# A new order of all queues in the opening fifth of a fused kernel: gated linear attention, then a feed-forward with hardswish

## The chip, the core and the metric

The kernel runs on one core of one Trainium2 chip. The core has five engines that run side by side and meet through semaphores: PE (TensorE, matmuls, with its weight loads as PEld), DVE (VectorE), ACT (ScalarE), POOL (GpSimd) and SP (SyncE, which here issues every DMA). Each engine takes its instructions strictly in the order in which the program gives them. The metric is the device time of one execution in microseconds (us); lower is better.

## The reference

The first block is a linear recurrence with a gate, for 4 batches x 8 heads, 768 steps, head size 48. Its output, seen as 3072 tokens x 384, goes through two matrices with hardswish between them. All inputs are float64 or float32 as given; the result is float32.

```python
def _attn_ref(q, k, v, alpha) -> np.ndarray:
    ...
    for t in range(S):
        state = alpha[:, :, t, :, None] * state + np.einsum('bhd,bhe->bhde', k[:, :, t], v[:, :, t])
        y[:, :, t] = np.einsum('bhd,bhde->bhe', q[:, :, t], state)
...
def _moe_ref(x, w_in, w_out) -> np.ndarray:
    h = x @ w_in                      # 3072 x 384 by 384 x 2048
    relu6 = np.clip(h + 3.0, 0.0, 6.0)
    g = h * relu6 / 6.0
    return (g @ w_out).astype(np.float32)
```

## The kernel before

**Tiling.** The sequence is cut into 24 chunks j of 128 tokens, six to a batch. Two chunks make a group g of 256 tokens, the unit of the feed-forward; there are 12 groups. The decay within a chunk is turned into scans along time, after which a chunk needs masked scores, a product with v, and a state carried to the next chunk. Groups 0 and 1 use plain matmuls for the first matrix (steps f, fa, fb), group 0 for the second too (b); from group 1's second matrix (steps s, x, P, K, G) and group 2's first matrix (steps y, xc, M, n, o) on, products of sums of blocks take their place, with fewer matmuls and more additions on DVE. The sums of weight blocks (x for w2, y for w1) are made once, in place, near the end of the opening.

**Steps and order.** All work is written as small functions, each under a short name in the dictionary `steps` (line 729), and one long list of words, passed to `run` (line 745), calls them one after the other: `d3.6` is `high_bits(6)`. Under the manual schedule an engine's queue is the order of that list, restricted to the instructions for that engine. Dependencies (a tile read after it was written, a buffer written again after its last reader) become semaphore waits, at which the whole queue behind them stands.

**The steps that matter here**, with the engine and the line of their costly instruction in the kernel before:

- Loads on SP: la, lk, lq (alpha, k, q of a chunk; L251 for chunks 0 to 5, into three ring buffers each; L262, four DMAs a chunk, from chunk 6 on, into two buffers "quads" each), lv (v, two DMAs, L272), w (one of 16 slices of the two weight matrices, L162 or L166).
- Weights, slice i: d2 (ACT, L196), d1 (ACT, L186), dx (ACT, L191, slices 0, 1, 2, 4 alone), d3 (DVE, two or three instructions: L203 and L205, or L207, L208 and L210), d4 (POOL, L217, which reads what d3, d1 and dx wrote). A slice's raw buffer is loaded again for a later slice once its d4 has read it.
- Chunk j: ta, tk, tq are PE transposes (L282) for chunks 0 to 5; from chunk 6 on tk, tq and ca are 32x32 transposes on DVE (L286). ca places alpha (ACT, L300, chunks 0 to 5), r and p are the scans (DVE, L309 and L320), k and q multiply (DVE, L332; out of PSUM for chunks 0 to 5, out of SBUF from 6 on), kb and ck turn k on PE and copy it (L374, L378), sc and m are scores and mask (PE L346, DVE L356), u, sm, st, sv the state (PE L429, DVE L439, POOL L409, ACT L419), qa places q (ACT, L366), ya, yb, cy the output of attention (PE L455, ACT L464).
- Feed-forward: f, fa, fb (PE, L478 and L489), fr and fg the gate (ACT L494, DVE L498), b (PE, L516), bo and so copy and store it; s (DVE, L647 and L664) and x (DVE, L647) are sums, P (PE, L703) the products, K and G copies and sums of them (ACT L682, DVE L719 or ACT L716), O the stores (L724); y (DVE, L537 to L541), xc (same lines), M (PE, L600), n (ACT, L606), o (DVE).
- z issues matmuls of the identity whose result nobody reads (PE, L532).

**Buffers.** Eight PSUM banks: t0 to t3 for attention, m0 to m3 for the feed-forward; the last number of a PE step's word is its bank, and a bank is free once ACT or DVE has read it. Three raw buffers (and two borrowed ones for slices 3 and 4) hold weight slices; sums y overwrite them later.

**Padding.** From chunk 6 on, loads into a quads buffer leave a corner of 32 x 64 elements of two partition blocks unwritten. The first load of each of the six buffers (a, k, q, two each) sets it to 1.0 with two memsets on POOL (L257), just ahead of its DMAs.

Of the kernel before, what the change touches and what calls it, by code (L numbers as in the profile page):

```python
# [17 lines left out]
def kernel(  # L18
# [228 lines left out]

    def load_akq(name, j):
        src = rows({"a": alpha, "k": k, "q": q}[name], j)
        if j < FIRST:  # L250
# [4 lines left out]
        if j < FIRST + NQ:
            for o in (BLK, 3 * BLK):
                nc.gpsimd.memset(to[o : o + BLK, :, V - 1, D - BLK : BLK], 1.0)  # L257
# [463 lines left out]
    def store2(g, i):  # L721
# [8 lines left out]
        "lq": lambda j: load_akq("q", j), "lv": load_v, "w": load_weight,  # L730
# [19 lines left out]
    with tc.manual_schedule():  # L750
        run("""z.0.5 z.0.3 z.0.1 z.0.8 qa.0.0 w.0 d2.0 d3.0 la.0 ta.0.0 ca.0 r.0 lk.0 tk.0.1 k.0
               z.0.2 p.0 la.1 ta.1.2 lq.0 tq.0.3 ca.1 r.1 lk.1 lv.0.0 sv.0.0 d1.0 kb.0.0 ck.0 z.0.2
               u.0.2.1 sm.0.0 sv.0.1 q.0 qa.0.1 tk.1.0 k.1 p.1 z.0.2 sc.0.2.3 m.0 la.2 ta.2.0 ca.2
# [179 lines left out]
```

## Time and profile before

| | us |
|---|---|
| Median of 3 runs | 533.65 |
| Lowest and highest | 533.3 and 533.85 |
| The profiled execution's own time | 533.84 |
| Its span, first to last instruction | 531.8 |
| PE busy | 522.2 |
| DVE busy | 477.0 |
| ACT busy | 257.4 |
| POOL busy | 50.4 |

A row of the timeline gives the start in us from the span's start, the duration in us, engine, line, operation, tiles, shape and count; in square brackets stands how long the engine had been idle before it and what ended that. In the chain the columns are start, duration and what. "PE m_ps L600" is a matmul into a bank of the feed-forward, issued in line 600. A matmul's duration includes its way through the array, so rows overlap; the distance between starts is what PE needs for one.

The profile names lines, not steps. Since every engine keeps the order of the list, the n-th instruction of an engine in the trace belongs to the n-th in the program, and so each row can be given its step.

### The profile page before, as it was taken

The page shows a single profiled execution, that of the slowest core. Times are in us where ns is not written, and L with a number is a line of the kernel's source. Part 1 is how long each engine was busy: PE and PEld are TensorE (multiplying, and loading weights), DVE is VectorE, ACT ScalarE, POOL GpSimd, SP SyncE. Part 2 cuts the span into 40 slices and gives each one's busy share as a digit, 9 for nine tenths or more (in the row PEclk, how much of TensorE's full clock was granted, in tenths as well). Part 3 has the DMA queues.
Part 4 walks back from the last instruction along what each step waited for, and adds up shares of the span by engine and source line. Part 5 has one row for each costly group of instructions (what it writes and reads, how often), then busy time and mean ns, then how long its engine had stood idle before and what let it go on. Part 6 is the DMA issues. An engine that isn't in the chain of part 4 may idle for free.

```text
span 531.8 us, 15143 instructions
## 1 busy us (share of the span) xinstructions
PE 522.2 (98%) x6306; PEld 496.9 (93%) x6306; DVE 477.0 (90%) x849; ACT 257.4 (48%) x503; POOL 50.4 (9%) x71
## 2 busy tenths in 40 slices
PE   7799999999999999999999999999999999999997
PEld 7698886789999999999999999999999999999997
DVE  6999989999999999999999999999999899496382
ACT  3889865212653553553544444642634544553340
POOL 5333425100000000000000000000000000000000
PEclk9999999999999999999999999999999999999999
DMA  9998887006615156254345356055364052100001
GB/s 173 218 254 247 211 231 156 18 2 149 155 31 118 30 125 139 49 137 100 89 107 118 90 123 143 18 134 111 92 138 105 10 110 44 44 2 2 15 16 37
DMA packets 124100, 54.40 MB, mean 102 GB/s; under 512 B 83328, under 2 KB 116864, under 8 KB 124032
## 3 DMA queue, kind: packets, MB, share of 16 engines
q1 hardware_dynamic: 124032, 53.44, 44.0%
q8 instruction: 49, 0.80, 0.7%
q14 instruction: 19, 0.16, 0.1%
HBM read 44.50 MB, written 8.91 MB: 100 GB/s over the span
## 4 chain that ended last, share of the span: by engine, by line
PE 81%; DVE 9%; ACT 3%; DMA 3%; POOL 2%; issue 1%; SPq 0%; DVEq 0%; POOLq 0%; ACTq 0%
PE m_ps L703 34%; PE m_ps L600 34%; PE m_ps L478 4%; PE t_ps L455 3%; PE t_ps L346 2%; PE t_ps L429 2%; DMA v<-in_v_dram 1%; DMA raw<-in_moe_w_out_dram 1%; DVE rings L647 1%; DVE R L309 1%; DVE raw L537 1%; ACT raw L186 1%; DVE g_sb L647 1%; ACT raw L191 1%; DVE w L537 1%
## 5 line engine op out<-in xcount | busy, mean ns | idle before, releaser
L606 ACT COPY g_sb<-m_ps 128x512 f32<-128x512 f32 x110 | 63.6, 584 | 123.7 <-PE m_ps L600 104.3
L703 PE MATMUL m_ps<-w,g_sb 128*128 128x192 f32 x704 | 121.7, 327 | 0.0
L703 PEld LDWEIGHTS m_ps<-w,g_sb 128*128 128x128 f32 x704 | 113.7, 190 | 0.4
L703 PE MATMUL m_ps<-rings,g_sb 128*128 128x192 f32 x528 | 91.5, 326 | 0.0
L703 PEld LDWEIGHTS m_ps<-rings,g_sb 128*128 128x128 f32 x528 | 85.4, 190 | 0.1
L600 PE MATMUL m_ps<-xc,w 128*128 128x128 f32 x640 | 82.8, 277 | 0.4 <-DVE w L541 0.4
L600 PEld LDWEIGHTS m_ps<-xc,w 128*128 128x128 f32 x640 | 77.5, 192 | 1.7 <-issue 0.6
L494 ACT ACTIVATE r<-g_sb,half 128x512 f32<-128x512 f32 x80 | 56.8, 722 | 33.1 <-DVE g_sb L541 12.1
L498 DVE SCALAR_TENSOR_TENSOR g_sb<-r,g_sb 128x512 f32<-128x512 f32 x80 | 53.7, 683 | 4.3 <-ACT r L494 3.9
L600 PE MATMUL m_ps<-xT,raw 128*128 128x128 f32 x400 | 52.5, 277 | 0.0
L600 PEld LDWEIGHTS m_ps<-xT,raw 128*128 128x128 f32 x400 | 48.6, 192 | 0.6
L409 POOL TENSOR_TENSOR st<-sm,R 128x192 f32<-128x192 f32 x20 | 12.9, 643 | 352.2 <-DVE sm L439 305.5
L647 DVE TENSOR_TENSOR g_sb<-g_sb 128x512 f32<-128x512 f32 (+1 forms) x55 | 41.9, 792 | 0.2
L600 PE MATMUL m_ps<-xT,w 128*128 128x128 f32 x320 | 42.0, 276 | 0.0
L600 PEld LDWEIGHTS m_ps<-xT,w 128*128 128x128 f32 x320 | 39.3, 192 | 0.1
L366 ACT COPY A<-q 48x256 f32<-48x256 f32 x88 | 35.6, 404 | 5.0 <-DVE q L332 3.8
L356 DVE TENSOR_TENSOR A<-t_ps,mask 64x256 f32<-64x256 f32 x96 | 36.0, 413 | 0.4
L478 PE MATMUL m_ps<-xT,w 128*128 128x256 f32 x144 | 32.8, 382 | 0.1
L600 PE MATMUL m_ps<-xc,raw 128*128 128x128 f32 x240 | 31.8, 276 | 0.0
L309 DVE TENSOR_TENSOR_SCAN R<-t,ones 128x516 f32<-128x516 f32 x24 | 29.6, 1235 | 1.0 <-ACT t L300 0.9
L478 PEld LDWEIGHTS m_ps<-xT,w 128*128 128x128 f32 x144 | 26.7, 190 | 3.8 <-POOL w L217 0.2
L600 PEld LDWEIGHTS m_ps<-xc,raw 128*128 128x128 f32 x240 | 29.6, 192 | 0.1
(104 smaller groups left out, 725.8 us busy)
## 6 DMA issues: line engine op xcount, KB each, us to landing
raw<-in_moe_w_out_dram SPq DMA_DIRECT2D x8, 768.0 KB, 5.3
raw<-in_moe_w_in_dram SPq DMA_DIRECT2D x6, 768.0 KB, 6.6
v<-in_v_dram SPq DMA_DIRECT2D x48, 96.0 KB, 3.1
out_dram<-oh SPq DMA_DIRECT2D x44, 96.0 KB, 1.7
far<-kq SPq DMA_DIRECT2D x64, 64.0 KB, 2.2
kb<-far SPq DMA_DIRECT2D x64, 64.0 KB, 2.1
aq<-in_alpha_dram SPq DMA_DIRECT2D x36, 96.0 KB, 2.7
qq<-in_q_dram SPq DMA_DIRECT2D x36, 96.0 KB, 2.5
```

What stands on the lines that cost most here:

```text
L309: nc.vector.tensor_tensor_scan(out=reverse(R, n - 1, n), data0=reverse(ax, n, n), data1=reverse(ones, n, n), initial=0.0, op0=ALU.mult, op ...
L356: nc.vector.tensor_tensor(out=to[:, a], in0=sc[a][half], in1=mask[half, half].unsqueeze(1).to_broadcast([HB, NP, HB]), op=ALU.mult)
L366: nc.scalar.copy(out=to[:, a], in_=Q_t[j][64 * a : 64 * a + D, :, half])
L409: nc.gpsimd.tensor_tensor(out=st, in0=sm, in1=R_t[j][:, :, 0:1].to_broadcast([C, NP, D]), op=ALU.mult)
L455: nc.tensor.matmul(y_of(j, (i + 1) // 2, p)[:, HB * b : HB * b + HB], vb[:, p, e : e + 32], A_t[j][:, b, 2 * p + a], start=(b == 0 and i = ...
L478: nc.tensor.matmul(h[:, f], w1[:, kk, o : o + C], xT_t[g][:, kk], start=(kk == 0), stop=(kk == KT - 1))
L494: nc.scalar.activation(out=to, in_=h, func=AF.Relu, bias=half, scale=1.0 / 6.0)
L498: nc.vector.scalar_tensor_tensor(out=to, in0=r, scalar=1.0, in1=h, op0=ALU.min, op1=ALU.mult)
L600: nc.tensor.matmul(acc[g][i][:, f * C : (f + 1) * C], spots[w][:, f * C : (f + 1) * C], x_of(g, x), start=(first and f == 0), stop=last, s ...
L606: nc.scalar.copy(out=slots[z], in_=acc[g][i])
L647: nc.vector.tensor_tensor(out=out, in0=in0, in1=in1, op=ALU.subtract)
L703: nc.tensor.matmul(to[g], a, rhs[:, f], start=(first and f == 0), stop=(last and f == HF - 1), skip_group_check=True)
```

## The change

The list of words is the same up to two new ones, pd.0 and pd.1; its order changes in the first 600 of some 1790 words, and nowhere behind them. The strongest changes lie ahead of M.2.0, the first product of group 2 (word 385 in both); behind it only loads, stores, three small steps (y.14, xc.2.0, qa.6.1) and, near word 590, O.1.0 with two steps beside it stand elsewhere. The memsets of the padding leave `load_akq` and become the step `pad(r)`: six memsets for the three buffers of number r, once for each r. Behind `pad`, all later line numbers are higher by 2.

```diff
@@ -245,6 +245,11 @@
         b, c = divmod(j, NC)
         return t[b, :, c * C : (c + 1) * C, :]
 
+    def pad(r):
+        for name in "akq":
+            for o in (BLK, 3 * BLK):
+                nc.gpsimd.memset(quads[name, r][o : o + BLK, :, V - 1, D - BLK : BLK], 1.0)
+
     def load_akq(name, j):
         src = rows({"a": alpha, "k": k, "q": q}[name], j)
         if j < FIRST:
@@ -252,9 +257,6 @@
                               in_=src.rearrange("h s d -> s h d"))
             return
         to = quads[name, j % NQ]
-        if j < FIRST + NQ:
-            for o in (BLK, 3 * BLK):
-                nc.gpsimd.memset(to[o : o + BLK, :, V - 1, D - BLK : BLK], 1.0)
         to = to.rearrange("r p v d -> r p (v d)")
         t = src.rearrange("(p a) (u v) d -> a u p (v d)", a=2, v=V)
         for o in range(4):
@@ -727,7 +729,7 @@
 
     steps = {
         "la": lambda j: load_akq("a", j), "lk": lambda j: load_akq("k", j),
-        "lq": lambda j: load_akq("q", j), "lv": load_v, "w": load_weight,
+        "lq": lambda j: load_akq("q", j), "lv": load_v, "pd": pad, "w": load_weight,
         "d1": round_low, "d2": magnitude, "dx": sign, "d3": high_bits, "d4": add_low,
         "ta": lambda j, *i: transposed("a", j, *i), "tk": lambda j, *i: transposed("k", j, *i),
         "tq": lambda j, *i: transposed("q", j, *i), "ca": place_alpha, "r": decay, "p": growth,
```

The list, old (-) and new (+), up to the words behind M.2.1:

```diff
-run("""z.0.5 z.0.3 z.0.1 z.0.8 qa.0.0 w.0 d2.0 d3.0 la.0 ta.0.0 ca.0 r.0 lk.0 tk.0.1 k.0
-       z.0.2 p.0 la.1 ta.1.2 lq.0 tq.0.3 ca.1 r.1 lk.1 lv.0.0 sv.0.0 d1.0 kb.0.0 ck.0 z.0.2
-       u.0.2.1 sm.0.0 sv.0.1 q.0 qa.0.1 tk.1.0 k.1 p.1 z.0.2 sc.0.2.3 m.0 la.2 ta.2.0 ca.2
-       dx.0 w.2 d2.2 kb.1.0 ck.1 lq.1 r.2 sm.0.1 st.1 tq.1.2 q.1 d3.2 z.0.3 d1.2 dx.2 lv.1.1
-       u.1.3.1 sv.1.0 sm.1.0 p.2 sm.1.1 sc.1.0.2 m.1 ya.0.3 yb.0 cy.0 lq.2 w.1 d1.1 tq.2.1
-       q.2 d4.2 lk.2 tk.2.3 k.2 fa.2.0 d4.0 st.2 sc.2.0.2 d2.1 d3.1 m.2 dx.1 d4.1 qa.1.1
-       lk.3 la.3 ta.3.1 ca.3 la.4 fa.0.1 sv.1.1 w.3 r.3 ta.4.3 ca.4 r.4 tk.3.1 k.3 kb.2.0
-       qa.1.0 d2.3 ya.1.2 yb.1 cy.1 fa.1.2 lq.3 ck.2 d1.3 p.3 d3.3 lv.2.2 u.2.3.2 sm.2.0
-       d4.3 fb.2 tq.3.1 q.3 fb.1 qa.2.0 sm.2.1 sv.2.0 st.3 fr.0.2.0 fg.0.2 lk.4 tk.4.0
-       sv.2.1 w.5 d2.5 k.4 d3.5 d1.5 qa.3.0 d4.5 qa.2.1 sc.3.1.3 m.3 w.6 d2.6 d1.6 d3.6 d4.6
-       lv.3.0 lq.4 w.7 kb.3.2 fb.0 f.0.3.3 kb.4.0 ya.2.1 ck.3 u.3.3.2 sm.3.0 fr.0.3.1 fg.0.3
-       fr.0.1.0 fg.0.1 qa.3.1 sv.3.0 sm.3.1 p.4 d2.7 sv.3.1 d1.7 d3.7 d4.7 f.0.5.0 fr.0.5.1
-       fr.0.0.0 fg.0.5 fg.0.0 tq.4.3 ck.4 la.5 ta.5.2 f.0.6.3 ca.5 w.4 d2.4 ya.3.0 yb.3 cy.3
-       fr.0.6.1 yb.2 cy.2 w.9 d2.9 q.4 qa.4.1 d1.4 d1.9 dx.4 la.6 w.8 d3.4 r.5 lk.5 w.10
-       d3.9 p.5 ca.6 fg.0.6 d4.9 w.12 lq.5 lv.4.1 d2.8 d3.8 f.0.7.2 d1.8 st.4 d4.8 d4.4 w.11
-       fr.0.7.0 fg.0.7 f.1.7.0 fr.1.7.1 fg.1.7 sc.4.0.2 m.4 f.1.1.1 fr.1.1.0 fg.1.1 f.1.3.3
-       fr.1.3.1 d2.10 d1.10 tk.5.3 f.1.0.2 d2.12 d3.10 d4.10 w.13 fg.1.3 fr.1.0.0 fg.1.0 k.5
-       d3.12 lq.6 f.1.6.0 f.1.2.1 u.4.1.0 sm.4.0 d1.12 d4.12 sv.4.0 qa.4.0 ya.4.2 fr.1.6.1
-       fg.1.6 w.15 tq.5.3 fa.4.3 sv.4.1 d2.11 kb.5.1 d2.13 fr.1.2.0 f.1.4.2 fr.1.4.1 d1.11
-       sm.4.1 q.5 r.6 d3.11 d3.13 fg.1.4 d4.11 lv.5.0 lk.6 tq.6 p.6 d2.15 d3.15 fg.1.2 d1.13
-       d4.13 sc.5.0.3 yb.4 f.1.5.0 fr.1.5.1 fg.1.5 tk.6 m.5 b.1.0.2 fb.4 b.1.1 d1.15 d4.15
-       st.5 y.5 w.14 la.7 lk.7 cy.4 d2.14 qa.5.1 ck.5 b.0.0.1 fr.0.4.0 d3.14 k.6 q.6 ca.7
-       fg.0.4 d1.14 d4.14 x.0 y.1 y.10 b.0.1 y.0 y.2 u.5.2 P.1.0.0 K.1.0 qa.5.0 sv.5.0
-       qa.6.1 P.1.1.3 b.0.2 b.1.2 kb.6.0 ya.5.3 y.6 s.1.0.0 sm.5.0 sv.5.1 G.1.0.0 tk.7
-       s.1.1.1 s.1.2.3 x.1 yb.5 cy.5 b.1.3 sc.6.1.2 lv.6.2 ck.6 u.6.3.0 s.1.3.2 x.2 P.1.2
-       b.0.3 K.1.1 y.7 s.1.4 s.1.5 y.11 y.3 r.7 xc.2.1 x.3 y.4 y.8 xc.2.3 k.7 xc.2.0 xc.2.4
-       y.9 y.12 y.16 y.13 y.15 P.1.3.3 K.1.2 P.1.4 bo.1 P.1.5 xc.2.5 G.1.1.1 P.1.6 y.14 y.17
-       y.19 xc.2.6 sm.6.0 G.1.2.2 y.20 M.2.0.2 lv.12.1 la.8 O.1.1 O.1.0 ca.8 y.18 y.21 y.23
-       so.1 G.1.3.3 n.2.0.8 bo.0 lq.7 lv.7.0 O.1.2 m.6 xc.2.2 xc.2.10 xc.2.7 tq.7 r.8 p.7
-       xc.2.8 sv.6.1 M.2.15.3 M.2.1 kb.7.3 n.2.1.9 M.2.16 M.2.2 n.2.2.10 M.2.7.0 n.2.7.11
...
+run("""z.0.5 z.0.3 z.0.1 qa.0.0 w.0 d2.0 d3.0 la.0 ta.0.0 z.0.8 la.1 lk.1 lk.0 tk.0.1
+       ta.1.2 lq.0 tq.0.3 lv.0.0 sv.0.0 d1.0 ca.0 r.0 p.0 k.0 kb.0.0 z.0.2 q.0 dx.0 ca.1
+       r.1 ck.0 u.0.2.1 sm.0.0 qa.0.1 tk.1.0 z.0.2 p.1 k.1 sc.0.2.3 w.2 la.2 ta.2.0 z.0.2
+       d2.2 sv.0.1 ca.2 kb.1.0 lq.1 sm.0.1 m.0 r.2 tq.1.2 q.1 z.0.3 d1.2 ck.1 dx.2 lv.1.1
+       u.1.3.1 sc.1.0.2 lk.2 w.1 lq.2 d4.0 st.1 sm.1.0 p.2 d3.2 sm.1.1 m.1 ya.0.3 yb.0 d4.2
+       w.3 la.4 la.3 lk.3 qa.1.0 cy.0 sv.1.0 st.2 d2.1 qa.1.1 d1.1 dx.1 fa.0.1 tq.2.1 q.2
+       tk.2.3 k.2 fa.2.0 sc.2.0.2 d3.1 m.2 d4.1 ta.4.3 ta.3.1 kb.2.0 d2.3 sv.1.1 ca.3
+       ya.1.2 yb.1 tk.3.1 cy.1 ca.4 fa.1.2 ck.2 d3.3 r.3 r.4 p.3 fb.2 lk.4 lq.3 lv.2.2
+       tk.4.0 u.2.3.2 sm.2.0 k.3 sm.2.1 w.5 qa.2.1 fr.0.2.0 sv.2.0 d1.3 d4.3 st.3 fg.0.2
+       d2.5 qa.2.0 k.4 d3.5 d1.5 d4.5 w.6 d1.6 d2.6 w.7 fb.0 fb.1 tq.3.1 q.3 d3.6 d4.6
+       kb.4.0 kb.3.2 f.0.3.3 sc.3.1.3 ck.3 fr.0.1.0 sv.2.1 fr.0.3.1 fg.0.3 m.3 d2.7 d3.7
+       fg.0.1 f.0.5.0 f.0.6.3 lk.5 lq.4 lv.3.0 u.3.3.2 ya.2.1 sm.3.0 sv.3.0 d1.7 qa.3.1
+       d4.7 ck.4 qa.3.0 fr.0.5.1 sv.3.1 fr.0.0.0 fg.0.5 sm.3.1 p.4 fg.0.0 la.5 ya.3.0
+       fr.0.6.1 yb.2 yb.3 ta.5.2 tq.4.3 cy.2 ca.5 q.4 pd.0 r.5 f.0.7.2 tk.5.3 lk.7 w.8 w.9
+       la.6 lq.5 w.4 d2.8 cy.3 qa.4.1 d3.8 ca.6 sc.4.0.2 f.1.1.1 f.1.7.0 qa.4.0 d2.9 d3.9
+       d1.8 d1.9 d4.9 st.4 d4.8 fr.0.7.0 d2.4 d1.4 dx.4 k.5 fg.0.6 fg.0.7 d3.4 fr.1.7.1 m.4
+       p.5 fr.1.1.0 tq.5.3 f.1.3.3 r.6 pd.1 d4.4 lv.6.2 lk.6 lv.4.1 w.10 w.12 w.11 d2.10
+       d1.10 u.4.1.0 f.1.0.2 sm.4.0 fg.1.7 fr.1.3.1 d1.12 d2.12 sv.4.0 sv.4.1 kb.5.1
+       f.1.6.0 sm.4.1 lv.5.0 lq.6 tk.6 fg.1.3 fa.4.3 fb.4 ck.5 d2.11 d1.11 k.6 d3.12 fg.1.1
+       d3.10 fr.1.0.0 fg.1.0 f.1.2.1 d4.12 d4.10 ya.4.2 fr.1.2.0 q.5 d3.11 d4.11 yb.4
+       sc.5.0.3 m.5 st.5 cy.4 fr.1.6.1 fg.1.6 u.5.2 f.1.4.2 kb.6.0 f.1.5.0 tk.7 p.6 fg.1.2
+       b.0.0.1 b.0.1 la.8 w.15 d2.15 la.7 w.13 w.14 ck.6 fr.1.4.1 fg.1.4 d3.15 b.1.0.2
+       fr.0.4.0 d2.13 d1.15 d4.15 qa.5.0 sv.5.0 d1.14 d2.14 d1.13 fr.1.5.1 ya.5.3 sm.5.0
+       tq.6 d3.13 d4.13 q.6 y.5 ca.7 d3.14 fg.1.5 fg.0.4 d4.14 y.10 y.1 x.0 s.1.0.0 sv.5.1
+       qa.5.1 yb.5 cy.5 sc.6.1.2 u.6.3.0 b.1.1 P.1.0.0 K.1.0 P.1.1.3 b.1.2 b.0.2 x.1
+       s.1.1.1 s.1.4 xc.2.1 x.2 G.1.0.0 y.2 y.6 s.1.2.3 y.7 s.1.3.2 P.1.2 K.1.1 y.3 y.11
+       y.9 x.3 y.8 y.4 xc.2.3 y.13 y.16 s.1.5 P.1.3.3 K.1.2 P.1.4 P.1.5 b.1.3 b.0.3 bo.1
+       G.1.1.1 y.15 r.7 xc.2.4 P.1.6 y.17 k.7 xc.2.5 y.19 xc.2.6 y.0 sm.6.0 G.1.2.2 y.12
+       y.20 M.2.0.2 ca.8 y.18 y.21 y.23 G.1.3.3 n.2.0.8 O.1.2 so.1 bo.0 lq.7 m.6 y.14
+       xc.2.0 xc.2.2 xc.2.10 xc.2.7 tq.7 r.8 p.7 xc.2.8 sv.6.1 M.2.15.3 M.2.1 kb.7.3
+       n.2.1.9 qa.6.1 M.2.16 M.2.2 n.2.2.10 M.2.7.0 n.2.7.11 sm.6.1 xc.2.9 q.7 p.8 M.2.3
...
```

In words: on PE, z.0.8 goes behind ta.0.0, fa.0.1 ahead of tq.2.1, fb.0 and fb.1 closer together, kb.4 and kb.3 ahead of f.0.3, ya.3, yb.2 and yb.3 together, b.1.3 from ahead of P.1.2 to behind P.1.5, and kb.6, sc.6, u.6 ahead of P.1.0. On DVE, r.3 and r.4 go behind d3.3; d3.5 and d3.6 stand with only q.3 between them; r.5, k.6, tk.6 and tk.7 come earlier, d3.4 later; x.1, x.2 and s.1.4 go ahead of s.1.2.3. On SP, la.1 and lk.1 go ahead of lk.0, w.2 ahead of la.2, w.3 ahead of la.4 and la.3, lk.7 to the place behind la.5, w.8 and w.9 ahead of la.6, la.8 ahead of la.7; lv.12, lv.7, O.1.0 and O.1.1 go behind M.2.1. On POOL, d4.0 goes ahead of d4.2, d4.9 and st.4 ahead of d4.8 as before but behind pd.0, and d4.4 behind pd.1. Word 590 and after: the old list has `P.2.5 G.2.2.0 st.9 M.3.12 sc.9.0.1 qa.8.0 n.3.12.10 o.3.3.0 kw.9 lv.9.0 kr.9`, the new one `P.2.5 st.9 M.3.12 sc.9.0.1 qa.8.0 n.3.12.10 kw.9 lv.9.0 kr.9 O.1.0 G.2.2.0 o.3.3.0`.

## The prediction

> **What bounds the kernel now.** First the shares of busy time and the chain that ended last.
>
> ```profile
> PE 522.2 (98%) x6306; PEld 496.9 (93%) x6306; DVE 477.0 (90%) x849; ACT 257.4 (48%) x503; POOL 50.4 (9%) x71
> ...
> PE 81%; DVE 9%; ACT 3%; DMA 3%; POOL 2%; issue 1%; SPq 0%; DVEq 0%; POOLq 0%; ACTq 0%
> ```
>
> PE is nearly always busy and is 81% of the chain; the rest lies in the opening. So I read the chain in order of time for the place where it becomes PE for good.
>
> ```profile
> 126.32 0.70 DVE raw L537
> 127.05 0.70 DVE w L541
> 127.75 0.14 issue
> 127.89 1.13 PE m_ps L600 x8
> ```
>
> The last combination of w1 (step y.23, L541) releases the third product of the next stage (M.2.1) at 127.89 us. After it PE waits for DVE nowhere up to 400 us, so whatever moves M.2.1 moves the end by as much. Next, the timeline of PE and of DVE ahead of that point.
>
> ```profile
> 106.08 2.85 PE L516 MATMUL m_ps<-w,g_sb 128*128 128x384 f32 x8
> ...
> 109.84 2.87 PE L703 MATMUL m_ps<-rings,g_sb 128*128 128x192 f32 x16
> ...
> 125.52 1.05 PE L600 MATMUL m_ps<-xc,raw 128*128 128x128 f32 x8
> 126.41 1.06 PE L600 MATMUL m_ps<-xT,raw 128*128 128x128 f32 x8
> 127.89 0.35 PE L600 MATMUL m_ps<-xc,w 128*128 128x128 f32 x1 [0.42 <-DVE w L541]
> ```
>
> ```profile
> 103.66 0.66 DVE L647 TENSOR_TENSOR g_sb<-g_sb 128x512 f32<-128x512 f32 x1
> 104.24 1.74 DVE L647 TENSOR_TENSOR w<-w 128x1536 f32<-128x1536 f32 x1
> 105.91 0.68 DVE L647 TENSOR_TENSOR g_sb<-g_sb 128x512 f32<-128x512 f32 x1
> 106.50 1.75 DVE L647 TENSOR_TENSOR rings<-w 128x1536 f32<-128x1536 f32 x1
> ```
>
> Here the two engines are level: PE would have been ready at 126.41 + 0.89 = 127.30. Product P.1.2 (109.84) reads s.1.2, s.1.3 and x.2, all ready by 108.2, so it is not late now. The step of an instruction is found by counting along each engine's queue. Lastly the places where DVE loses time: its waits, and its rows beside POOL's (excerpts).
>
> ```profile
> 1.47 6.67 PE L532 MATMUL m_ps<-ident 128*128 128x128 f32 x34 [1.47 <-POOL ident masks.py:199]
> 7.97 1.04 PE L282 MATMUL t_ps<-ident,rings 128*128 128x128 f32 x8
> 8.84 0.61 PE L532 MATMUL m_ps<-ident 128*128 128x128 f32 x4
> 9.22 1.23 DVE L309 TENSOR_TENSOR_SCAN R<-t,ones 128x516 f32<-128x516 f32 x1 [0.94 <-ACT t L300]
> ```
>
> ```profile
> 81.73 2.02 POOL L217 TENSOR_TENSOR w<-raw 128x768 int32<-128x768 int32 x1 [0.17 <-POOL kq L257]
> 82.40 1.77 DVE L207 TENSOR_SCALAR w<-w 128x768 f32<-128x768 f32 x1
> ...
> 92.40 1.69 POOL L217 TENSOR_TENSOR w<-raw 128x768 int32<-128x768 int32 x1 [3.73 <-DVE raw L210]
> 92.69 1.96 DVE L332 TENSOR_TENSOR q<-q,P 128x512 f32<-128x512 f32 x1
> ```
>
> ```profile
> 72.48 0.36 DVE L439 TENSOR_TENSOR s<-t_ps,st 128x192 f32<-128x192 f32 x1 [1.14 <-PE t_ps L429]
> ```
>
> The middle fence carries most of this forecast. An L207 usually takes 0.62 us; behind a running POOL L217 (step d4) it took 1.77 and ended 0.42 after it. The k/q multiply L332 takes 0.60; with both inputs in SBUF and behind a d4 it took 1.96. In all of the opening, DVE work that reads PSUM (fg, m, sm, q and k of the first six chunks) and 32x32 transposes lose nothing beside a d4; tensor_scalars and two-input SBUF work (scans, r.3 +0.40, d3.1 +0.32) stand still until it ends. And a d4 that finds DVE inside such an instruction waits, then goes ahead of DVE's next. So the instruction behind each d3 decides: d3 releases its d4 some 0.13 us after it ends, and a d4 runs 1.47 us (1.85 for slices 0, 1, 2 and 4).
>
> **The change part by part.** The sum goes by DVE's queue up to s.1.2.3, because the new order puts P.1.2 ahead of b.1.3 on PE.
>
> *Work moved past the point.* In the old order s.1.2.3 is over at 104.24. The new order has x.1 and x.2 (1.67 each), s.1.4 (1.14) and xc.2.1 (0.18) in front of it and y.0 (0.60) behind: +4.06, so 108.30 if DVE lost as much as before.
>
> *What DVE stops losing.* z.0.8, sixteen matmuls of padding ahead of ta.0.0, goes behind it. The first alpha landed by 6.93, ta.0.0 ran at 7.97; now it runs at about 7.0 and the first scan goes straight behind d3.0, at 8.31 instead of 9.22: -0.91. The waits of 0.28 (sm.0.0) and 1.14 (sm.4.0, whose update u.4 comes earlier) go, and so do the lock losses at d3.1 0.32, r.3 0.40, d3.15 1.15, q.6 1.28. Together -5.48.
>
> *What it loses anew, early.* On SP la.1 and lk.1 pass lk.0, and lq.0 is one place later. Loads land in queue order (la.0 6.93, then 8.16, 9.36, 10.55, 12.01), so k.0, now next in DVE's queue, waits 0.5 and q.0 0.6; r.1, sm and p.1 stand behind them. The update u.1 still waits for lv.1, which lands at 20.02 in both orders: DVE, early there, waits 0.3. By m.2 (29.4 in both) the early scan is spent: +1.4.
>
> *Locks in new places.* The price is the end of the d4 less DVE's arrival less 0.13. Two worked out: d3.5 now ends near 40.75, d4.5 runs from 40.88 to 42.35, and only q.3 (0.60) stands between d3.5 and d3.6, so L207 of d3.6 arrives at 41.35 and loses 0.9 (in the old order m.3, 1.5 long and out of PSUM, stood there). At y.5, q.6 is ahead of the waiting d4.13, which then goes first: 1.35 less 0.13, 1.25. The others in the same way: d3.3 behind d4.1 0.4; d3.5 behind d4.3 0.3; d3.4 behind st.4 0.2 and behind d4.8 1.25; p.5 behind d4.4 0.4; d3.10, with fg.1.1 alone between, behind d4.12 0.9; d3.11 behind d4.10 and d3.13 behind d4.15 0.3 each; y.10 behind d4.14 0.3. That is 6.5. Three of them (d4.8, y.5, y.10; 2.8) hang on which engine asks first, by 0.3 us or less; between nothing and 2.8 no row is nearer to the one than to the other, and I take half: 5.1.
>
> *Waits for PE.* With fa, fb and the transposes in another order, u.2, u.3 and tq.4 come 0.35, 0.2 and 0.45 after DVE asks for them: +1.0.
>
> Sum: 1.4 + 5.1 + 1.0 - 5.48 = +2.0, so s.1.2.3 ends at 110.3 and P.1.2 starts at 110.4. From there to M.2.1 PE took 127.30 - 109.84 = 17.46; b.1.3, now inside that stretch, adds 2.69: 110.4 + 20.15 = 130.55, against 127.89: **+2.7 us**. PE by itself would be at P.1.2 at 107.2 (109.84 less b.1.3) if it never waited; it does wait, because m.5, fg.1.6 and fg.1.2, which free banks for kb.6, f.1.5 and b.0.0, now stand behind transposes of chunks 6 and 7 on DVE.
>
> *Edits that cost nothing.* Twelve memsets of 0.14 (pd.0, pd.1) leave the loads and run on POOL between d4s; la.6 waits for pd.0 (about 50) and is wanted by ca.6 at 57; lk.7 passes ahead of pd.1, whose region it doesn't touch. d4.4 waits behind pd.1 (0.9), covered by fa.4, ten us later. SP has the same 472 issues; w.8 and w.9 go ahead of la.6, lk.7 comes some 37 us early, la.8 and lv.6 too, into tiles long free; without that cover u.4, due at 65, would wait for lv.4, which I put at 61. y.14 and xc.2.0 (0.80) go behind y.23: worth -0.80 to DVE's end, which at 129.5 is under PE's 130.55. qa.6.1 goes into ACT's idle 1.64 us behind n.2.1.9. O.1.0 goes behind kr.9 (171.2), and G.2.2.0, which reuses its buffer, is due at 179.57: 6 us to spare; lk.11 behind it is 0.4 later, with no reader before 190. lv.12 and lv.7.0 land long before their chunks.
>
> *The clock.* The first 34 padding matmuls took 6.67 us: 213 ns apart until 6.97 us, 112 after, and the four at 8.84 are 112 apart. So the switch came after 5.5 us of unbroken matmuls (from 1.47). In the new order PE idles from 5.7 to 7.0. If the switch counts from there again, it comes as late as 12.5: z.0.8 and tk.0 then run at 213, and k.0 sees tk.0 1.0 us later; of that lv.1 takes up half or nothing: +0.5 to +1.0 on the end. If it doesn't, nothing is lost. I take 0, as a gap of 1.3 us in 5.5 is small, and give the other end a rival of its own. [...]
>
> Base: the profiled execution took 533.84 with a span of 531.8, 0.19 over the median of 533.65. On the median: 533.65 + 2.7 = 536.35, or **536.4 us**.
>
> **The rivals.**
> *Faster: PE sets the end.* If few d4s meet locking work, DVE is done with s.1.2.3 by 107 and y.23 by 126, and PE only has to run through. PE then keeps what it gains before 40 us (fa.0 fills a gap of 0.44 at 23, the 0.33 at 30.3 goes) and the 0.58 before M.2.1: about -1.6, 532.0. For it: PE's own idle time in the opening, about 16 us beside its nominal spacing, is smaller in the new order. It decides below a net DVE loss of -1.7. Against: d3.6 and d3.10 meet their d4s whatever else shifts. Chance 0.19.
> *About the same: the moves cancel.* A net loss on DVE near -0.7 instead of +2.0 gives 533.65. For it: both orders have the same work, and half of the locks are small. Chance 0.17.
> *Slower by more: every contested lock is lost.* +2.0 + 1.4 on DVE gives +4.1 at M.2.1: 537.8. For it the row of q.6, where POOL, asking second, still went ahead. Chance 0.09.
> *The clock stays at half until 12.5.* 536.35 + 1.0: 537.4. Against it the gap is short. Chance 0.06.
> *Nothing reordered* is excluded: every queue differs.
>
> **How the numbers follow.** Forecast 0.49, every lock 0.09, clock 0.06, same 0.17, faster 0.19. 0.2%, 1.07 us, is about what a measurement of this kernel can tell from no change. Slower by over that: 0.64; within: 0.17; faster: 0.19. The range runs from the PE-bound 532.0 to every lock and the slow clock together, 538.8. Cases of both signs are in it; the likeliest one's own, with the contested locks at nothing and at full, is 535.0 to 537.8.
>
> **What would show it.** First L309 scan at 8.3 (right) or later than 9 (clock); L332 waiting for lk.0 near 11; m.2 near 29.4; L207 (now L209) at 1.3 us or more in d3.6 and d3.10; the x16 L703 group of P.1.2 starting at 110 to 111 with idle before it; the first L600 at 128 to 129. If L207 shows its usual 0.62 there, or P.1.2 starts at 107.5, the forecast is wrong and the first rival right. After M.2.1 the trace should be the old one, shifted.

## The result, and the profile after

The changed kernel takes 539.28 us (median of 4 executions, 538.77 to 540.06) against 533.75 us of the kernel before beside it: 1.0106 times as long, 95% interval 1.0088 to 1.0123, or 5.5 us more where the prediction had 2.7 more. The profiled execution took 538.77 with a span of 536.9, 5.1 more than the old span. Two of the four executions, the profiled one among them, took 538.8 us and the other two 539.8 and 540.1; no trace here shows why.

The busy times of the engines and the row of the instruction queue, from the page of the changed kernel:

```profile
PE 521.9 (97%) x6306; PEld 495.8 (92%) x6306; DVE 481.6 (90%) x849; ACT 257.6 (48%) x503; POOL 49.0 (9%) x71
...
q8 instruction: 49, 0.80, 0.6%
```

PE has the same work; DVE is busy 4.6 us longer with the same 849 instructions. An instruction that stands still counts as busy (rows below show it: d3.6 is one row of 1.54 us for a usual 0.69), so this difference is already a hint at the locks: DVE instructions that wait until a running POOL instruction ends. The second line becomes important below: 49 packets, 0.80 MB; that they hold PE's code is concluded there from counts and times.

The chain that ended last, in order of time (start, duration, what), around the place where it becomes PE for good:

```profile
112.28 0.61 DVE g_sb L649
112.89 0.14 issue
113.03 10.73 PE m_ps L705 x64
123.75 5.16 PE m_ps L518 x16
```

In the old kernel the chain went over from DVE to PE at y.23 and M.2.1. Now it does so at 113.03: s.1.2.3 (L649) releases P.1.2 (L705), and from there PE runs without a stop. The two timeline rows of PE that matter:

```profile
113.03 1.70 PE L705 MATMUL m_ps<-rings,g_sb 128*128 128x192 f32 x9 [0.97 <-DVE g_sb L649]
...
133.13 1.10 PE L602 MATMUL m_ps<-xc,w 128*128 128x128 f32 x8
```

From P.1.2 to M.2.1 it takes 20.10 us; the prediction had 20.15. M.2.1 starts 5.24 later than before, and behind it PE's rows are the old ones, shifted by 5.1 to 5.2 (P.11.5, near the end, starts 5.15 later). So everything that is to be explained lies ahead of 113 us.

With the usual durations of the old trace, DVE's queue up to the end of s.1.2.3 can be added up for both kernels:

| us | before | after | difference | predicted |
|---|---|---|---|---|
| work | 89.47 | 93.54 | +4.07 | +4.06 |
| time over the usual durations (mostly locks) | 4.07 | 8.23 | +4.16 | +1.95 |
| idle | 4.03 | 4.46 | +0.43 | +0.07 |

The last column is made of the prediction's terms: 5.1 of new locks less 3.15 of old ones; 1.4 and 1.0 of new waits less 2.33 of old ones. (They leave out what is ahead of the first step on DVE, 6.7 and 6.6 us.) The locks are 2.2 us more than forecast, the waits 0.4. Three of the lock rows (POOL's d4 beside DVE, timeline):

```profile
40.95 1.47 POOL L217 TENSOR_TENSOR w<-raw 128x768 int32<-128x768 int32 x1 [2.62 <-DVE raw L210]
...
41.42 1.54 DVE L207 TENSOR_SCALAR w<-w 128x768 f32<-128x768 f32 x1
...
66.88 1.84 POOL L217 TENSOR_TENSOR w<-w,g_sb 128x768 int32<-128x768 int32 x1
...
67.51 2.30 DVE L322 TENSOR_TENSOR_SCAN P<-t 128x516 f32<-128x516 f32 x1
...
95.29 1.60 POOL L217 TENSOR_TENSOR w<-raw 128x768 int32<-128x768 int32 x1 [2.33 <-ACT raw L186]
...
95.48 1.96 DVE L543 SCALAR_TENSOR_TENSOR raw<-w 128x512 f32<-128x512 f32 x1
```

The same d3.6 and p.5 in the old order, where no d4 holds them up:

```profile
42.91 0.69 DVE L207 TENSOR_SCALAR w<-w 128x768 f32<-128x768 f32 x1
...
57.09 1.23 DVE L320 TENSOR_TENSOR_SCAN P<-t 128x516 f32<-128x516 f32 x1
```

The first pair is d4.5 beside d3.6: 0.86 lost, 0.9 predicted. The second is d4.4 beside p.5, whose scan usually takes 1.22: 1.08 lost, 0.4 predicted. The third is d4.13 beside y.5, which usually takes 0.69: about 1.28 lost, where the prediction counted half of 1.25.

The idle time hides the second surprise. DVE waits 1.83 us ahead of q.4, not the 0.45 predicted, and this is why (timeline):

```profile
49.63 1.77 PE L457 MATMUL t_ps<-A,v 128*32 128x64 f32 x106
...
52.99 0.54 PE L457 MATMUL t_ps<-A,v 128*32 128x64 f32 x22 [1.58 <-issue]
...
54.58 0.69 DVE L334 TENSOR_TENSOR q<-t_ps,P 128x512 f32<-128x512 f32 x1 [1.83 <-PE t_ps L284]
```

PE stops for 1.80 us between two matmuls of the same step (yb.3; 106 matmuls of ya.2, ya.3, yb.2 and yb.3 ahead of it, 22 behind), and "issue" says that the profile knows no engine or DMA that it waited for. In the old order the 96 matmuls of ya.3, yb.3 and yb.2 run through (timeline of the kernel before):

```profile
50.64 1.55 PE L455 MATMUL t_ps<-A,v 128*32 128x64 f32 x96
```

### The profile page after: what moved, and what is told of

It is laid out like the page before. It is cut to its first block, busy times and chain, and to the rows that moved or that the text cites. A ratio compares the mean times of both kernels' runs of the same rounds, so it can differ in the third digit from the quotient of the medians.

```text
span 536.9 us, 15129 instructions
## 1 busy us (share of the span) xinstructions
PE 521.9 (97%) x6306; PEld 495.8 (92%) x6306; DVE 481.6 (90%) x849; ACT 257.6 (48%) x503; POOL 49.0 (9%) x71
## 4 chain that ended last, share of the span: by engine, by line
PE 81%; DVE 11%; DMA 2%; issue 2%; SPq 1%; ACT 1%; POOL 1%; DVEq 0%; POOLq 0%
PE m_ps L705 37%; PE m_ps L602 34%; PE t_ps L457 4%; PE t_ps L348 2%; PE t_ps L431 2%; DVE w L207 1%; PE m_ps L480 1%; DVE w L208 1%; DVE g_sb L500 1%; PE m_ps L518 1%; DMA rings<-in_k_dram 1%; DVE raw L210 1%; DVE R L311 1%; DMA kq<-in_k_dram 1%; SPq L256 1%
## 5 line engine op out<-in xcount | busy, mean ns | idle before, releaser
L705 PE MATMUL m_ps<-w,g_sb 128*128 128x192 f32 x704 | 121.6, 327 | 0.0
L705 PEld LDWEIGHTS m_ps<-w,g_sb 128*128 128x128 f32 x704 | 113.7, 190 | 0.5
L705 PE MATMUL m_ps<-rings,g_sb 128*128 128x192 f32 x528 | 91.4, 326 | 1.0 <-DVE g_sb L649 1.0
L705 PEld LDWEIGHTS m_ps<-rings,g_sb 128*128 128x128 f32 x528 | 85.4, 190 | 1.9 <-issue 1.6
L649 DVE TENSOR_TENSOR g_sb<-g_sb 128x512 f32<-128x512 f32 (+1 forms) x55 | 42.0, 794 | 0.3
L322 DVE TENSOR_TENSOR_SCAN P<-t 128x516 f32<-128x516 f32 x24 | 30.4, 1265 | 0.1
```

Source lines behind the costliest of these rows:

```text
L322: nc.vector.tensor_tensor_scan(out=P_t[j], data0=aX[j % 2][:, 0:n], data1=ini[j % 2], initial=0.0, op0=ALU.mult, op1=ALU.add)
L649: nc.vector.tensor_tensor(out=out, in0=in0, in1=in1, op=ALU.subtract)
L705: nc.tensor.matmul(to[g], a, rhs[:, f], start=(first and f == 0), stop=(last and f == HF - 1), skip_group_check=True)
```

## The experiments

The reasons to be told apart were three. LOCK: what DVE loses beside d4 in its new places. CODE: the pause, taken as PE waiting for its next block of instructions. ORDER: PE's waits for other reasons, and the work moved ahead of s.1.2.3. "After" below is the changed kernel; each edit is made to it unless said otherwise. Every ratio is to the kernel before, run beside it on the same chip.

**1. Short work on POOL in place of d4 (e1_after_soft).**

```diff
-nc.gpsimd.tensor_tensor(out=dst.bitcast(I32), in0=high.bitcast(I32), in1=lo.bitcast(I32), op=ALU.add)
+few = lambda t: t.bitcast(I32)[:, 0:1, 0:16]
+nc.gpsimd.tensor_tensor(out=few(dst), in0=few(high), in1=few(lo), op=ALU.add)
+nc.gpsimd.memset(dst[:, :, 16:], 0.015625)
+nc.gpsimd.memset(dst[:, 0:1, 16:], 0.015625)
```

> The changed kernel, with each d4 (the add of the low bits on POOL) replaced by a 16-column add and two memsets that keep POOL busy for about as long. It leaves out the low bits and overwrites most weights by a constant, so only its time is to be read. Theory LOCK (what DVE loses beside d4 in its new places is most of the loss): the rows of d3.3, d3.6, d3.4, p.5, d3.10 and y.5, now 0.8 to 1.3 us over their usual length, go back to it; s.1.2.3, over at 112.8 in the changed kernel, is over near 105; PE then sets P.1.2, which goes from 113.0 to about 108.6, and M.2.1 from 133.1 to about 128.7: 534.9 us, between 533.5 and 536. Rival ORDER (PE's own waits and the work moved ahead of s.1.2.3 are the loss, the locks lie beside other work): P.1.2 not before 112, 538 us or more. Both expect PE's pause of 1.8 us inside yb.3 to stay.

Measured: 534.33 us, ratio 1.0013 (1.0001 to 1.0025). Its timeline at d3.6 and at P.1.2:

```profile
41.41 0.69 DVE L207 TENSOR_SCALAR w<-w 128x768 f32<-128x768 f32 x1 [0.36 <-ACT w L196]
...
108.07 2.76 PE L707 MATMUL m_ps<-rings,g_sb 128*128 128x192 f32 x16
```

Beside a memset in the same place d3.6 takes its usual 0.69, s.1.2.3 starts at 106.61 instead of 112.20, P.1.2 at 108.07 without a wait, M.2.1 at 128.01. PE's pause in yb.3 is still there (1.85). So the locks decide, and with short ones PE makes up for most of what is left, the pause included. ORDER alone is ruled out as the main cause.

The substitute does not take every lock away. POOL is held by parts of 0.2 to 0.7 us instead of 1.47 or 1.85, and a tensor_scalar still waits for a running memset, as the first instruction of d3.10 does here (0.90; in the changed kernel 1.50, in the kernel before 0.56):

```profile
73.66 0.71 POOL L219 MEMSET w<- 128x736 f32 x1
73.89 0.90 DVE L207 TENSOR_SCALAR w<-w 128x768 f32<-128x768 f32 x1
```

At d3.6 DVE was first and the memset waited (0.58 us instead of 0.30). Scans and work with two inputs in SBUF lose nothing beside the memsets (p.5 takes 1.23, y.5 0.70).

**2. The same in the old order (e5_before_soft).** The edit of e1 in the kernel before.

> The kernel before, with the same substitute for d4 as in the run e1_after_soft (low bits left out, weights overwritten; only its time is to be read). It asks what the locks cost in the old order. Theory LOCK AND BOUND: DVE loses 4.1 us less up to s.1.2.3, but PE, which waits for DVE only 0.58 us ahead of M.2.1 and little before, sets the end: M.2.1 goes from 127.89 to about 127.2, 533.1 us. So the old order pays next to nothing for its locks, the new one 5 us. Rival: the locks delay PE's early steps in the old order as well: 531.5 or less.

Measured: 532.65 us, ratio 0.9983 (0.9973 to 0.9992). M.2.1 starts at 126.64, 1.25 earlier: more than the 0.7 expected, since the early steps gain too (q.4 starts 1.1 us earlier already), and less than the rival's 2.3. So with this substitute the old order gains 1.2 us (533.82 less 532.65) and the new one 5.0 (539.28 less 534.33): the difference, 3.8, is most of the 5.5. In both orders this is the gain of shorter locks, not of none: here d3.15 still took 1.17 beside a memset of 0.71.

**3. b.1.3 back ahead of P.1.2 (e2_p12).**

```diff
-... y.7 s.1.3.2 P.1.2 K.1.1 ... P.1.5 b.1.3 b.0.3 ...
+... y.7 s.1.3.2 b.1.3 P.1.2 K.1.1 ... P.1.5 b.0.3 ...
```

> The changed kernel with b.1.3 put back ahead of P.1.2 on PE; nothing else is moved. Theory CHAIN (DVE's s.1.2.3 keeps PE from P.1.2, and PE then runs without a stop to M.2.1): the 1.13 us that PE waits ahead of P.1.2 are covered, M.2.1 goes from 133.13 to 132.0, just behind y.23 (131.43): 1.1 us off, 538.2. Rival: the wait only moves, since K.1.1, bo.1 or y.23 come later too: under 0.4 us off, 538.9 to 539.5.

Measured: 539.86 us, ratio 1.0113 (1.0098 to 1.0128): nothing gained, the rival is right. PE no longer waits for s.1.2.3, but P.1.4 comes 1.0 us later, and DVE's G.1.1.1, which adds its result, now stands 1.18 us with y.15 to y.23 queued behind it: y.23 is over at 132.32 instead of 131.43 and PE waits 1.0 us for it ahead of M.2.1. M.2.1 is still 0.67 earlier than in after, in part because the pause was shorter in this trace (0.95); PE loses that again at M.2.8, which stands for xc.2.8, over 0.9 later on DVE. Both engines are level, and moving PE's work alone only moves the wait.

**4. The border of the code shifted, no step moved (e3_shift).**

```diff
+def tiny(n):
+    for _ in range(n):
+        nc.tensor.matmul(bank_m[0][0:32, 0:32], ident[:, 0:32], ident[:, 0:32], start=True, stop=True)
...
-z.0.8 la.1 ... sc.0.2.3 w.2 ... yb.0 d4.2
+z.0.8 zz.11 la.1 ... sc.0.2.3 zz.11 w.2 ... yb.0 zz.10 d4.2
```

> The changed kernel with 32 tiny matmuls (two instructions each for the weights and the data, in two passes: 128 instructions) whose result nobody reads, in three places before 23 us where PE is idle. No step changes its place. Theory CODE (the pause of 1.80 us in the middle of yb.3, at matmul 727 of the trace, is PE waiting for its next 16 KB of instructions, which it asks for when it enters the block before): the border of the block falls 64 matmuls earlier in the work, at the start of ya.3; the block is asked for in sc.3.1.3, some 8 us ahead, and the pause goes; q.4 starts near 53.0 instead of 54.58, and M.2.1 is 1.4 us earlier: 537.9. Rival DATA (yb.3 waits for something that an engine or a DMA writes): the pause stays where it is, 539.3.

Measured: 542.57 us, ratio 1.0162 (1.0147 to 1.0177). PE's timeline rows:

```profile
28.04 2.50 PE L491 MATMUL m_ps<-xT,w 128*128 128x128 f32 x10 [3.54 <-issue]
...
55.71 1.99 PE L457 MATMUL t_ps<-A,v 128*32 128x64 f32 x128
```

The pause in yb.3 is gone: ya.2 to yb.3 are one unbroken run of 128 matmuls. That is what CODE said and DATA excludes, since no step or buffer changed there. But another border came to lie in a step that ran through before, fa.0.1, and PE stood there for 3.70 us. Between q.3 (6.07 later than in after) and q.4 (4.19 later) the run regains 1.88, the price of the old pause, and keeps it up to M.2.1 (4.19 later). A second pause of this kind, 0.99 us in sc.4.0.2, added nothing there.

**5. Other work between the small steps (e4_spread).**

```diff
-f.0.5.0 f.0.6.3 lk.5 lq.4 lv.3.0 u.3.3.2 ya.2.1 sm.3.0
+f.0.5.0 lv.3.0 u.3.3.2 ya.2.1 f.0.6.3 lk.5 lq.4 sm.3.0
```

> The changed kernel with u.3 and ya.2 put ahead of f.0.6 on PE, and the load of v of chunk 3, which u.3 reads, ahead of lk.5 and lq.4. So the 256 instructions of u.3, ya.2, ya.3 and yb.2 don't follow each other at once, but with f.0.6 (2.9 us) between. Theory CODE: the pause in yb.3 goes, PE's wait of 0.85 ahead of f.0.6 is filled, q.4 starts near 53.1, M.2.1 1.4 us earlier: 537.9. Rival DATA: the pause stays, q.4 not before 54, 539 us.

Measured: 538.85 us, ratio 1.0099 (1.0082 to 1.0116); q.4 starts at 54.55, as in after (54.58). The pause is down to 0.56, but u.3 now stands 1.34 us for its bank, which m.3 frees at 47.3. A miss: PE's wait of 0.85 ahead of f.0.6 was no time that u.3 could use.

**6. The border shifted where PE is idle later (e6_shift2).** The tiny matmuls of 4, now into bank m3:

```diff
-tq.3.1 q.3 d3.6 ... f.0.5.0 f.0.6.3
+tq.3.1 zz.3.7 q.3 d3.6 ... f.0.5.0 zz.3.10 f.0.6.3
```

> The changed kernel with 17 tiny matmuls (68 instructions) whose result nobody reads, in the two places after 37 us where PE is idle anyway (0.55 us ahead of kb.4, 0.85 ahead of f.0.6); no step moves. Theory CODE: the block border in yb.3 falls 34 matmuls earlier, to the end of ya.3; the block is asked for at the end of sc.3.1.3 near 42.7 and is there by 50; the pause of 1.80 us goes, nothing ahead of 37 us changes, q.4 starts near 52.8, M.2.1 comes 1.6 to 1.9 us earlier: 537.5. Rival: the pause is not on the path that sets the end: M.2.1 as before, 539.3.

Measured: 537.42 us, ratio 1.0066 (1.0050 to 1.0082), against 539.28. In the profiled execution (538.01) a pause of 0.51 is left, now in yb.2, 34 matmuls earlier in the work, as the shift says; M.2.1 is 0.7 earlier. e8_best, e9_best2 and e12_shift_pad below, with the same shift, have no pause in their traces.

**7. Cover beside the d4s (e7_relock).** The essential words:

```diff
-fg.0.7 d3.4 fr.1.7.1 m.4 p.5 ... pd.1 d4.4
+fg.0.7 m.4 d3.4 fr.1.7.1 d4.4 fg.1.7 ... tk.6 p.5 ... pd.1
-tq.3.1 q.3 d3.6
+tq.3.1 q.3 fg.0.1 d3.6
-fg.1.1 d3.10
+fg.1.1 tq.6 d3.10
-sm.5.0 tq.6 d3.13 d4.13 q.6 y.5 ca.7 d3.14 fg.1.5 fg.0.4 d4.14 y.10
+sm.5.0 tk.7 d3.13 d4.13 ca.7 fg.0.4 q.6 y.5 d3.14 fg.1.5 d4.14 ca.8 y.10
...
-d2.1 qa.1.1 d1.1 dx.1 ... d1.14 d2.14 d1.13
+d2.1 d1.1 dx.1 qa.1.1 ... d1.13 d1.14 d2.14
```

> The changed kernel with full d4s, and beside six of them work on DVE that reads PSUM or turns 32x32 blocks, in place of work that locks: m.4 goes ahead of d3.4, fg.1.7 and tk.6 between d3.4 and p.5, fg.0.1 ahead of d3.6, tq.6 ahead of d3.10, tk.7 ahead of d3.13, ca.7 and fg.0.4 ahead of q.6, ca.8 ahead of y.10; on ACT dx.1 and d1.13 one place earlier, fr.0.1 earlier; pd.1 goes behind d4.4. Theory LOCK: the losses in the rows of d3.3, d3.6, d3.4, p.5, d3.10, y.5 and y.10 fall from 5.9 us to about 1.5, ca.8 adds 0.96 ahead of s.1.2.3: s.1.2.3 3 to 4 us earlier, M.2.1 near 129.6, 535.8 us (535 to 537). Rival ORDER: another wait takes their place: 538 or more.

Measured: 536.56 us, ratio 1.0056 (1.0042 to 1.0070). With every d4 in full, DVE's time over the usual durations up to s.1.2.3 falls from 8.23 to 3.24, M.2.1 comes 2.5 us earlier. The first part of the gain is lost: d3.3 and d3.6 take 1.0 us less, but then DVE waits 0.65 for u.3 ahead of sm.3.0, the pause in yb.3 was 2.10 us this time, and q.4 started at 54.53, as in after.

**8. Locks, code and s.1.2.3 together (e8_best).**

```diff
-x.1 s.1.1.1 s.1.4 xc.2.1 x.2 G.1.0.0 y.2 y.6 s.1.2.3 y.7 s.1.3.2 P.1.2 K.1.1
+x.1 s.1.1.1 x.2 s.1.2.3 s.1.3.2 G.1.0.0 s.1.4 xc.2.1 y.2 y.6 y.7 P.1.2 K.1.1
```

> The run e7_relock, with the 17 tiny matmuls of e6_shift2, and s.1.2.3 and s.1.3.2 straight behind x.2 (s.1.4, xc.2.1, y.2, y.6 and y.7 behind them). If lock and code are the whole loss and add, PE sets P.1.2 and M.2.1 comes near 127: 533, level with the kernel before or up to 1 us faster. If it stays above 535, a third cause is in the new order.

Measured: 534.98 us, ratio 1.0021 (1.0012 to 1.0030). No pause; s.1.2.3 starts at 104.97, P.1.2 at 109.12 with no wait ahead of it. The three edits together bring back 4.3 of the 5.5 us. Something else is in the new order: s.1.3.2 is over 2.8 us ahead of P.1.2, so PE is late by itself, and it had stood 1.59 us ahead of kb.5.

**9. The third cause (e9_best2).** On top of 8, sm.4.0 goes ahead of p.5 and r.6.

> The run e8_best with sm.4.0 ahead of p.5 and r.6 on DVE (the update u.4 that it reads goes ahead of them in the list). In e8_best PE sets the end: nothing on DVE keeps it from P.1.2 any more, and it stands 1.59 us ahead of kb.5, whose bank sm.4.0 frees. Theory THIRD CAUSE: this wait, 1.19 us in the changed kernel and nothing in the old one, is what is left; P.1.2 goes from 109.1 to about 107.6, M.2.1 from 129.1 to 127.5: 533.4 us, level with the kernel before (0.3 less to 0.3 more). Rival: PE waits elsewhere instead, 534.6 or more.

Measured: 534.13 us, ratio 1.0009 (1.0000 to 1.0018). The wait ahead of kb.5 is gone, P.1.2 starts at 108.30 and M.2.1 at 128.24, later than the 127.5 expected, in part because PE then stands 0.73 us for q.5 ahead of sc.5. The new order is now level with the old one, within what can be measured.

**10. The padding (e10_pad; e12_shift_pad, with the shift of 6 as well).**

```diff
-r.6 pd.1 d4.4 lv.6.2
+r.6 d4.4 pd.1 lv.6.2
```

> The changed kernel with pd.1 behind d4.4 on POOL; nothing else is moved. The prediction had the memsets cost nothing. Theory PADS SHIFT A LOCK: d4.4 starts near 66.1 instead of 66.88 and ends near 67.95 instead of 68.72; the scan p.5, which asks at 67.5, loses 0.3 instead of 1.08; M.2.1 0.7 to 0.8 us earlier, 538.5. Rival: what p.5 gains is lost again in a wait (sm.4.0, kb.5): 539.0 to 539.5.

> The run e6_shift2 (537.42 us) with pd.1 behind d4.4 as in e10_pad, whose time the pause in yb.3 blurred. Theory PADS SHIFT A LOCK: p.5's row falls from 2.2 us to about 1.5, and what stands behind it keeps the gain, so M.2.1 is 0.6 to 0.7 us earlier than in e6_shift2 at the same q.4: 536.7. Rival: the gain is lost in a wait further on: 537.4.

Measured: 539.15 us (1.0097, 1.0082 to 1.0113) and 537.00 us (1.0064, 1.0050 to 1.0078). The first says nothing on the time: its trace has a pause of 2.17 us in yb.3, longer than after's 1.80. In the second, without any pause, p.5 takes 1.63 instead of 2.30, 0.67 less, and M.2.1 is 1.94 earlier than in after where q.4 is 1.49 earlier, so some 0.45 of it seem to reach M.2.1. The time does not show it: the ratios of e6_shift2 and of this run, 1.0066 and 1.0064, can't be told apart. The row of p.5 is clear, the price at the end is small and not shown.

**11. The old order with two locks covered (e11_before_relock).**

```diff
-p.6 d2.15 d3.15 fg.1.2 ... d3.14 k.6 q.6 ca.7 fg.0.4
+p.6 fg.1.2 d2.15 d3.15 ... d3.14 ca.7 fg.0.4 k.6 q.6
```

> The kernel before with two changes on DVE alone: ca.7 and fg.0.4 go ahead of k.6 and q.6, beside d4.14, and fg.1.2 goes ahead of d3.15, beside d4.13. Theory LOCK: q.6 no longer loses 1.28, d3.15 loses 0.6 instead of 1.15; y.23 is over 1.5 to 1.9 us earlier, PE no longer waits its 0.58 for it, M.2.1 goes from 127.89 to about 127.3: 533.2 us against 533.8 (533.0 to 533.5). Rival: PE is delayed elsewhere by as much: 533.7 or more.

Measured: 533.03 us, ratio 0.9988 (0.9980 to 0.9997), a little faster than both kernels, by less than the 0.2% bound. The row of q.6:

```profile
94.49 0.69 DVE L332 TENSOR_TENSOR q<-q,P 128x512 f32<-128x512 f32 x1
```

It took 1.96 before. PE no longer waits for y.23. In the profiled execution (533.67) M.2.1 is no earlier, since PE paused for 0.59 us in fb.2 near 34.5, at a block border again by the count below: the old order is not free of such pauses, only less exposed.

## Why the prediction was right and wrong

*Right: the place and the mechanism.* That new meetings of d3 and other locking work with d4 outweigh the old ones, that DVE's s.1.2.3 then keeps PE from P.1.2, that PE needs 20.15 from there, and that nothing is regained later. The first scan came at 8.27 (8.3 predicted), the work moved past s.1.2.3 was 4.07 (4.06). Experiments 1 and 7 show the locks at work. Experiment 3 adds what the prediction had only touched (DVE's end 1 us under PE's): behind P.1.2 y.23 is nearly as late, so giving PE its old order back gains nothing.

*Wrong: the size of the locks.* The step that failed is the sum of new lock losses, 5.1 us. The listed rows measure 6.74 (each duration less the usual one, 0.68 for a tensor_scalar):

| step | predicted | measured |
|---|---|---|
| d3.3 | 0.4 | 0.86 |
| d3.5 | 0.3 | 0.0 |
| d3.6 | 0.9 | 0.86 |
| d3.4, behind st.4 and d4.8 | 0.2 + 1.25 | 0.33 + 0.88 |
| p.5 | 0.4 | 1.08 |
| d3.10 | 0.9 | 0.82 |
| d3.11, d3.13 | 0.3, 0.3 | 0.16, 0.17 |
| y.5 | 1.25 | 1.28 |
| y.10 | 0.3 | 0.30 |

The three contested ones (d4.8, y.5, y.10) were all lost: 2.46 where half of 2.8 was taken. POOL, asking second, goes ahead of DVE's next instruction, as the row of q.6 in the old trace had shown; halving was a choice against that row. The other miss is p.5: the prediction let the memsets of pd.1 delay d4.4 by 0.9 and called it covered by fa.4. There it looked only at who waits for d4.4, not at how much longer p.5, already priced beside it at 0.4, would then stand. Experiment 10 shows 0.67 us for it. The table of the result has 2.2 us more of lost time than forecast; these rows make 1.6 of it, and the rest is spread over small differences that were not followed up.

*Wrong: tq.4 comes 0.45 us late.* It came 1.83 late. The prediction put u.3, ya.2, ya.3, yb.2 and yb.3, now in one row on PE, at their start-to-start costs. By the count of the last section they are, but for a few, one block of 256 PE instructions, executed in 2 us; PE then stood, and went on at 52.99, 1.31 us after the end of a packet of 16 KB (50.56 to 51.68). Experiment 4 shows that the pause moves with the count of instructions, not with the step; in e12_shift_pad, where the trace has no pause, q.4 is 1.49 earlier and M.2.1 with it. Nothing in the old trace showed such a pause, so it could not be priced there, but a bound could have been named.

*Off, without consequence: the early part.* m.2 ended at 28.94, not at 29.4. The pause set q.4, so the 0.5 us were lost again.

*The rivals.* "Every contested lock is lost" at 537.8 had the contested locks right, with a chance of 0.09; 537.8 and the unforeseen 1.4 at q.4 make 539.2. That this meets the measured time so well is partly luck, as p.5's other 0.7 and the 0.5 gained by m.2 are not in it. "The clock stays at half until 12.5" did not happen in after's trace (z.0.8 took 1.95, its matmuls 112 ns apart, though PE had worked only from 1.46 to 5.67 ahead of the gap), but did in the traces of experiments 4 and 9 (3.38 and 3.49, with the matmuls 213 ns apart until 11 us) and nearly so in that of e12_shift_pad (3.14); in 9 m.2 started only 0.1 later than in after, so the wait for lv.1 does take it up, as the prediction said. What these rows show is PE's pace: the granted clock in the records is 1.00 from 3 to 6 and from 7 to 12 us in before, after, 4 and 9 alike. "PE sets the end" is what experiments 8 and 9 reach, at 534 rather than 532. The new order has waits ahead of kb.5 (gone in 9) and sc.5 that the old one hasn't; that they are the whole reason is not shown.

*Edits that cost nothing.* True of the loads (DVE waits for no load of a weight, though w.14 landed at 89.8), y.14, xc.2.0, qa.6.1 and O.1.0; untrue of pd.1.

## What to carry to other kernels

When work is reordered, go through each long instruction of POOL and ask what DVE will execute while it runs: in these traces DVE instructions that read PSUM, or a 32x32 transpose, cost nothing beside an add on POOL (in after fg.0.6 and fg.0.7 took their usual 0.68 us beside d4.9, tq.6 1.13 beside d4.15 against 1.10 to 1.16 elsewhere), while a scan, a tensor_scalar or work with two inputs in SBUF waits for the rest of it (p.5 2.30 for 1.22, d3.6 1.54 for 0.69, y.5 1.96 for 0.69). Delaying the POOL instruction by a few small ones is not free if it then meets other work (0.67 us at p.5 in experiment 10). And count instructions, not only time: in after several steps of tiny matmuls in a row, together 256 instructions of PE, were executed in 2 us, and PE then stood for 1.80. A long matmul step between them made the pause shorter (1.80 to 0.56 us in experiment 5), but there the step that moved forward then waited for a bank.

## What the runs showed of the hardware

*Pauses of PE in bursts of small matmuls, and packets of 16 KB.* Both kernels have 49 packets of 16 KB (0.80 MB) on an instruction queue of their own, and PE executes 12,612 matmuls and weight loads: 257 a packet, or some 64 bytes for each. In the kernel before 6,029 matmuls lie between the starts of the first packet and of the last, 126 from one to the next. From this, and from the times below, the packets are taken for PE's code; the trace gives their kind, instruction, and names no engine. The packets' times are in the trace's list of DMA packets; put beside the pauses:

```
kernel            packet (us)      PE goes on at   pause   in step
after             50.56 - 51.68    52.99           1.80    yb.3
e1_after_soft     49.47 - 50.47    51.91           1.85    yb.3
e2_p12            49.72 - 51.21    52.58           0.95    yb.3
e4_spread         50.41 - 51.29    52.95           0.56    yb.3
e6_shift2         49.48 - 50.41    51.84           0.51    yb.2
e7_relock         50.49 - 51.42    52.93           2.10    yb.3
e10_pad           50.76 - 51.68    53.45           2.17    yb.3
e3_shift          25.17 - 26.63    28.04           3.70    fa.0.1
e3_shift          60.57 - 61.70    62.96           0.99    sc.4.0.2
e11_before_relock 32.45 - 33.95    35.17           0.59    fb.2
```

PE always goes on 1.2 to 1.8 us after the packet's end. Counted along PE's matmuls the pauses lie ahead of number 346, 471, 726 or 727, and 853: each 128 or 256, within 3, behind the one before it, and 128 matmuls with their weight loads are 256 instructions. In these ten cases the packet begins to move 0.0 to 4.3 us after PE entered the block before (counted out along PE's instructions), in a stretch where loads keep the DMA engines full (the profile's DMA share in the 4 us ahead of the packet is 0.92 to 1.21). That the packet waits behind these loads is inferred, not shown. In after that block was entered at 49.27 and used up in 2 us. That a packet is asked for when PE enters the block before, as the expectations of experiments 4 and 6 have it, was the author's estimate; the start of a packet is what the traces show.

*The clock after a pause.* After the 3.70 us of experiment 4 PE's matmuls were 213 ns apart. The stretch from 28 to 31.5 us of that run (the third number from the end is the granted clock):

```profile
28.00:31.50 3.50, 3.46 (x16) 3.46 (x17) 0.06 (x1) 2.40 (x4) 0.00 (x0) 0.51 1.09 174
```

From 24 to 28 us and from 31.5 to 40 it was 1.00. After 2.17 us in e10_pad it was 0.52 as well, from 54.0 to 57.5; after 2.10 us in e7_relock and 1.80 in after it stayed at 1.00. So of three pauses near 2 us one was followed by 3.5 us at half speed and two were not.

*What waits for POOL.* A DVE tensor_scalar that meets running work on POOL ends 0.41 to 0.55 us after that work, be it an add (d3.10 in after: the add ends at 78.30, DVE at 78.71) or a memset (d3.10 in experiment 1: 74.37 and 74.79). What it loses is the rest of the POOL instruction, so some 1.1 us at d3.15 in the kernel before (1.77 long, behind an add) and a few tenths beside the shorter memsets (0.90 long at d3.10 in experiment 1, 1.17 at d3.15 in experiment 2, for a usual 0.68). Scans and work with two inputs in SBUF lose up to 1.28 beside adds, which read SBUF, and nothing beside memsets, which only write it (y.5: 1.96 in after, 0.70 in experiment 1). At p.5, 1.08 us late, d4.4 ends 1.21 after p.5 asked.
